# Chunked attention and a channel mix on one core: a new order for the steps of the opening

## The chip, the cores and the metric

The kernel runs on one core of a Trainium2 chip. The metric is the device time of one execution in microseconds (us). The kernel before takes 577.14 us by the median of three runs (576.09 to 577.93). The engines are TensorE (PE, with its weight loads as PEld), ScalarE (ACT), VectorE (DVE), GpSimd (POOL) and SyncE (SP, which here issues nearly all loads and stores).

## The reference

Inputs q, k, v have the shape batch 8, heads 8, sequence 576, head size 64. The sequence is cut into chunks of 64, and each chunk attends to itself alone:

```
scores = q_c @ k_c.T / sqrt(64)              # 64 x 64 for each chunk and head
attn   = softmax(scores)                     # sum + 1e-9 in the denominator
x      = (attn @ v_c), heads side by side    # 8 x 576 x 512
x_prev = x shifted by one token, zero at the start of a batch
xk     = mu_k * x + (1 - mu_k) * x_prev;   xr likewise with mu_r
k      = relu(xk @ w_k)                      # 512 -> 1024
v      = (k * k) @ w_v                       # 1024 -> 512
out    = sigmoid(xr @ w_r) * v
```

## The kernel before

The 8 x 576 tokens are 4608 in a row, cut into 18 groups of 256 and 36 tiles t of 128. Every product of the channel mix is made in three passes over a high and a low part of each operand (`PASSES`, L612), so activations and weights have to be split: hi is a rounded copy, lo is the rest. The attention of groups 0 to 2 and the channel mix of groups 0 and 1 are called the opening here; it is written tile by tile, because the weights are still on their way. The groups behind it run from another list (`GROUP`), which the change leaves alone.

**How the order is set.** Each function of the opening registers small steps under a task name (`do`, class `Steps`); a step is called task.number. The string `START` (from L27) lists all steps in one order, with an engine behind a colon where there is a choice, and the loop at L1210 issues them in that order. Within each engine, and within SP's queue, instructions keep the order of the text. Semaphores between engines, and the waits for a free buffer of a pool, follow from the data. The engine letter counts only in steps that copy, subtract or apply relu and square on either engine; the passes over weights have fixed engines. `W:n` issues n idle products on PE, which have no reader.

**The steps**, with the lines where they are defined:

- `nq`, `nk` (L173): a group's q or k into a ring, 512 KB, on SP. `v` (L191): a tile's v, four loads, two buffers. `bq3`, `bk3` (L208): 16 small loads each of q or k for group 3, by 32-blocks.
- `swk`, `swr`, `swv` (L271): load of 1 MB of weights. `cw...` 0 and 1 are two ScalarE passes over it, 2 a combine on VectorE (they turn the stored words into fp32); `hw...` 0 is the copy to the high part, 1 the low part (a subtraction). wk has four such blocks, wr two, wv four; wv2 and wv3 share one buffer for the loaded words.
- `mu`, `dg` (L230, L526): the mix factors, and 16 diagonal matrices made from them on ScalarE.
- `T`g (L348): 0, 2 transpose q's even and odd tokens on PE, 4, 6 k's; 1, 3, 5, 7 copy them to `qT`, `kT`. The products go to the pool `ps_k`, two buffers of one bank, which `K` and `mu` use too.
- `S`t (L384): 0 scores on PE, 1 maximum, 2 subtraction (both read PSUM on VectorE), 3 exponential on ScalarE, 4 sum, epsilon and reciprocal, 5 division. Two tiles share one PSUM buffer (`ps_s`, one buffer of two banks, which `P`.0 uses in turn), and steps that touch the same bank wait for each other in the order of the text.
- `P`t (L456): 0 transposes the probabilities on PE, 1 copies them out, 2 multiplies with v, 3 fills the shifted column, 4 copies the result x out.
- `Mk`t, `Mr`t (L542): 0 difference, 1 mix (for t = 0, 1, 2 on PE with the diagonals, in pool `ps_o`; else on VectorE), 2 high copy, 3 low part (`Mr` has no step 0: 0 mix, 1 high, 2 low).
- `K`gf (L618): 0 the product with a block of wk (24 products), 1 relu, 2 square, 3 high, 4 low. `R`gt (L673): 0 the product with wr, 1 sigmoid. `V`g... (L699): products with wv, one step for each of eight row blocks, and the last steps multiply with the sigmoid and store.
- `D6`, `D7` (L377): VectorE turns the q (0) and k (1) blocks of group 3.

The pools that matter: `ps_k` 2 buffers, `ps_s` 1, `ps_x` 1 (results of P.2 for two tiles), `ps_o` 2 (mixes, R and V).

Of the kernel before, what the change touches and what calls it, by code (L numbers as in the profile page):

```python
# [24 lines left out]


START = """  # L27
W:9 mu.0:A nq0.0 nk0.0 T0.0 T0.2 T0.1:A swr1.0 P0.3:D T0.3:A nk1.0 nq1.0 T0.4 T0.5:A swr0.0
T0.6 T0.7:A W:4 S0.0 S0.1:D S0.2:D S1.0 W:4 T1.4 S1.1:D v0.0 T1.6 S1.2:D cwr1.1:A S0.3:A S0.4:D
S0.5:D cwr1.0:A T1.5:A W:3 T1.0 S1.3:A S1.4:D S1.5:D P0.0 T1.7:A cwr1.2:D T1.2 cwr0.0:D P1.0  # L30
T1.1:A mu.1 P0.1:A T1.3:A cwr0.1:A nq2.0 P0.2 P1.1:A S2.0 T2.2 S3.0 P0.4:D P1.3:D S2.1:D v1.0
S2.2:D mu.2:A dg.0:A S3.1:D T2.0 swk0.0 S2.3:A cwr0.2:D Mk0.1 S3.2:D T2.3:A P1.2 S2.4:D
hwr1.0:A Mk1.0:D Mk0.0:D nk2.0 Mk0.2:A cwk0.0:A swk2.0 S2.5:D Mr0.0 swk1.0 cwk0.1:A P1.4:A
T2.1:A S3.3:A T2.6 Mr0.1:A hwr1.1:D Mk0.3:D P2.3:D hwr0.0:A P2.0 cwk0.2:D Mr0.2:D Mk1.1 swk3.0
Mk1.2:A Mk1.3:D T2.7:A hwr0.1:D T2.4 Mr1.0 hwk0.0:D P2.1:A Mr1.1:D hwk0.1:D R00.0 cwk2.0:A
Mr1.2:D v2.0 S3.4:D cwk1.1:A T2.5:A Mk2.0:D cwk1.0:A swv2.0 S3.5:D v3.0 cwk1.2:D cwk3.1:A P2.2
R01.0 P2.4:A cwk2.1:A K00.0 swv0.0 R00.1:A P3.3:D R01.1:A cwk3.0:A cwk2.2:D P3.0 P3.1:A K00.1:A
hwk2.0:A Mr2.0 P3.2 hwk1.0:A cwk3.2:D Mr2.1:A S4.0 P3.4:A Mk2.1 hwk2.1:D S5.0 hwk1.1:D cwv2.0:A
cwv2.1:A hwk3.0:A swv1.0 K01.0 K01.1:A K01.2:A Mk3.0:D Mr3.0:D K02.0 K00.2:A cwv2.2:D hwk3.1:D
v4.0 Mk3.1:D Mr2.2:D S4.1:D Mr3.1:A K03.0 cwv1.1:A Mr3.2:D cwv1.0:A bk3.0 Mk2.2:D Mk2.3:D  # L40
K00.3:A R10.0 S5.1:D Mk3.2:A cwv0.1:A K01.3:A hwv2.0:A K00.4:D K02.1:A K02.2:A K01.4:D K02.3:A
P4.3:D cwv0.0:A R10.1:A Mk3.3:D hwv2.1:D R11.0 K03.1:A K02.4:D K03.2:A R11.1:A K10.0 K10.1:A
swv3.0 K10.2:A cwv0.2:D K11.0 cwv1.2:D hwv0.0:A K03.3:A S4.2:D K13.0 hwv1.0:A hwv0.1:D cwv3.1:A
bq3.0 S5.2:D cwv3.0:A K10.3:A K03.4:D v5.0 hwv1.1:D V001.0 cwv3.2:D S4.3:A K13.1:A V001.1
V001.2 hwv3.0:A K10.4:D V001.3 V001.4 S4.4:D K13.2:A S4.5:D V001.5 P4.0 hwv3.1:D S5.3:A V001.6
V001.7 P4.1:A S5.4:D K13.3:A S5.5:D P4.2 K11.1:A K13.4:D D7.1:D v7.0 P5.0 P4.4:A K11.2:A
V001.8:D K12.0 V10.0 V001.9:D V11.0 K11.3:A V11.1 P5.1:A Mk4.0:D Mk4.1:D K12.1:A P5.2 K12.2:A
P5.3:D K12.3:A K11.4:D V10.1 D6.1:D K12.4:D P5.4:A Mr4.0:D V10.2 V10.3 V11.2 V11.3 Mk5.0:D
V10.4 Mk5.1:D Mr4.1:A V11.4 D7.0:D Mk4.2:A V10.5 v6.0 V10.6 V11.5 V10.7 Mk5.2:A Mk4.3:D Mr4.2:D
Mk5.3:D Mr5.0:D Mr5.1:A V11.6 D6.0:D V11.7 V11.8:D Mr5.2:D V10.8:D  # L50
"""


# [1255 lines left out]
```

## Time and profile before

| what | value |
|---|---|
| median of three runs | 577.14 us (576.09 to 577.93) |
| the profiled execution | 577.38 us |
| its span, first to last instruction | 575.6 us |
| granted clock of TensorE, mean | 0.999 |
| DMA over the span | 49.25 MB, mean 86 GB/s |

All rows are of the profiled execution. Times in rows count from the start of its span. A row of a timeline merges neighbouring instructions of one kind; the length of a merged row reaches to the end of its last instruction, so that rows of a pipelined PE overlap by a little, and the distance from one start to the next is the cost of a step in a full queue.

### The profile page before, as it was taken

The numbers are of one execution on the slowest core, as the hardware profiler recorded it, in microseconds if no ns is written. First come the engines' busy times: TensorE is split into PE (matmuls) and PEld (weight loads), VectorE is DVE, ScalarE is ACT, GpSimd is POOL, SyncE is SP. The second block draws the span as 40 slices with busy tenths as digits, with TensorE's granted clock in tenths as the row PEclk, the third lists the DMA queues.
The fourth block names the chain that finished last, engine by engine and source line by source line (L and its number), as shares of the span: only waits on it lengthen the run. The fifth ranks groups of instructions, "written<-read, shape, count | busy, mean of one in ns | idle before, by whom it ended". The sixth has DMA issues, their size and how long they took to land.

```text
span 575.6 us, 15305 instructions
## 1 busy us (share of the span) xinstructions
PE 566.6 (98%) x6485; PEld 535.8 (93%) x6485; DVE 453.8 (79%) x763; ACT 356.2 (62%) x535; POOL 0.7 (0%) x6
## 2 busy tenths in 40 slices
PE   7899999999999999999999999999999999999997
PEld 7779999999999999999999999999999999999997
DVE  1686878889888888888888697979798878876835
ACT  4898975473848383929292929292938384747462
POOL 0000000000000000000000000000000000000000
PEclk9999999999999999999999999999999999999999
DMA  9997342433443343434203434343434343010011
GB/s 286 201 315 199 89 86 75 89 67 70 69 91 66 82 69 88 70 91 67 72 1 90 68 86 69 84 71 89 69 83 69 84 70 74 21 41 36 1 38 38
DMA packets 184276, 49.25 MB, mean 86 GB/s; under 512 B 169608, under 2 KB 176272, under 8 KB 184208
## 3 DMA queue, kind: packets, MB, share of 16 engines
q1 hardware_dynamic: 183904, 48.01, 37.1%
q8 instruction: 51, 0.84, 0.6%
q10 hardware_dynamic: 304, 0.27, 0.1%
q14 instruction: 17, 0.14, 0.1%
HBM read 38.80 MB, written 9.44 MB: 84 GB/s over the span
## 4 chain that ended last, share of the span: by engine, by line
PE 95%; DMA 3%; ACT 0%; SPq 0%; DVE 0%; issue 0%
PE pk L627 35%; PE pr L680 17%; PE vx L900 15%; PE vyz L900 11%; PE pv L711 6%; PE xps L1085 3%; PE s L1011 3%; PE pt L1067 2%; DMA v<-in_v 2%; PE trq L358 1%; DMA q_ring<-in_q 1%; PE mxk L571 1%; PE s L401 1%; PE trk L358 1%; PE xps L485 1%; PE warm L1214 1%
## 5 line engine op out<-in xcount | busy, mean ns | idle before, releaser
L627 PE MATMUL pk<-xkhi,wk 128*128 128x256 f32 x1152 | 202.2, 278 | 0.0
L627 PEld LDWEIGHTS pk<-xkhi,wk 128*128 128x128 f32 x1152 | 175.4, 188 | 1.2
L627 PE MATMUL pk<-xklo,wk 128*128 128x256 f32 x576 | 159.4, 277 | 0.0
L647 ACT ACTIVATE rr<-pk 128x512 f32<-128x512 f32 x60 | 35.3, 588 | 128.6 <-PE pk L627 128.6
L627 PEld LDWEIGHTS pk<-xklo,wk 128*128 128x128 f32 x576 | 108.3, 188 | 0.1
L680 PE MATMUL pr<-wr,xrhi 128*128 128x512 f32 x288 | 90.4, 395 | 0.0
L900 PE MATMUL vyz<-b,kk 128*128 128x256 f32 x540 | 68.7, 276 | 0.0
L900 PE MATMUL vx<-b,ks 128*128 128x256 f32 x540 | 68.7, 276 | 0.0
L900 PEld LDWEIGHTS vx<-b,ks 128*128 128x128 f32 x540 | 64.7, 188 | 0.0
L900 PEld LDWEIGHTS vyz<-b,kk 128*128 128x128 f32 x540 | 64.7, 188 | 0.0
L680 PEld LDWEIGHTS pr<-wr,xrhi 128*128 128x128 f32 x288 | 52.7, 188 | 10.2
L680 PE MATMUL pr<-wr,xrlo 128*128 128x512 f32 x144 | 56.2, 390 | 0.0
L738 DVE TENSOR_TENSOR kk<-rr,kk 128x1024 fp32r<-128x1024 f32 x30 | 35.4, 1222 | 11.2 <-ACT kk L884 11.1
L654 ACT ACTIVATE rr<-rr 128x512 f32<-128x512 f32 x60 | 38.0, 633 | 1.9
L929 ACT ACTIVATE u<-vx 128x256 f32<-128x256 f32 x30 | 11.5, 384 | 42.3 <-PE vx L900 42.3
L711 PE MATMUL pv<-b,kk 128*128 128x256 f32 x288 | 33.9, 277 | 0.0
L711 PEld LDWEIGHTS pv<-b,kk 128*128 128x128 f32 x288 | 33.1, 188 | 0.1
L680 PEld LDWEIGHTS pr<-wr,xrlo 128*128 128x128 f32 x144 | 27.0, 188 | 5.7
L846 DVE TENSOR_TENSOR ss<-rr 128x512 f32<-128x512 f32 x15 | 10.4, 692 | 24.7 <-ACT rr L654 24.7
L738 DVE TENSOR_TENSOR ks<-ss,ks 128x512 fp32r<-128x512 f32 x45 | 28.3, 685 | 0.0
L1147 DVE SCALAR_TENSOR_TENSOR mk<-d,mu,x 128x256 f32<-128x256 f32 (+3 forms) x80 | 27.6, 413 | 0.4
L1147 DVE SCALAR_TENSOR_TENSOR mr<-d,mu,x 128x256 f32<-128x256 f32 (+3 forms) x80 | 27.6, 412 | 0.0
(127 smaller groups left out, 864.0 us busy)
## 6 DMA issues: line engine op xcount, KB each, us to landing
v<-in_v SPq DMA_DIRECT2D x144, 64.0 KB, 2.4
out<-sg SPq DMA_DIRECT2D x34, 256.0 KB, 2.6
q_ring<-in_q SPq DMA_DIRECT2D x192, 36.0 KB, 2.0
k_ring<-in_k SPq DMA_DIRECT2D x192, 36.0 KB, 2.0
wk_st<-in_moe_w_k SPq DMA_DIRECT2D x4, 1024.0 KB, 12.8
wv_st<-in_moe_w_v SPq DMA_DIRECT2D x4, 1024.0 KB, 7.4
wr_st<-in_moe_w_r SPq DMA_DIRECT2D x2, 1024.0 KB, 10.1
q_ring<-in_q SPq DMA_DIRECT2D x2, 512.0 KB, 6.7
```

The lines of the kernel that those rows point to most:

```text
L358: nc.tensor.matmul(x[halves[j], hp, :], T[f"{nm}{g}"][:, j * HP + hp, r, :], ident, start=True, stop=True,)
L627: nc.tensor.matmul(pk[:, e, :], wk[a][:, cb, f * P : (f + 1) * P], xk[b][:, cb, :], start=(n == 0), stop=(n == 3 * NB - 1),)
L647: nc.scalar.activation(r, T[f"pk{g}{fp}"], AF.Relu)
L654: nc.scalar.activation(r, r, AF.Square)
L680: nc.tensor.matmul(pr, xr[a][:, cb, tl * TT : (tl + 1) * TT], wr[b][:, cb, :], start=(n == 0), stop=(n == 3 * NB - 1),)
L711: nc.tensor.matmul(T[f"pv{g}{tl}"][:, cols[c]], kk[a][:, f, tok[tl]], quarter(f // HF, c)[:, b, f % HF, :], start=(f == 0 and n == 0 and c ...
L738: nc.vector.tensor_tensor(to, x, y, ALU.subtract)
L900: nc.tensor.matmul(to, a[i][:, f, :], weight(w, j, f), start=first and f == 0 and n == 0, stop=f == HF - 1 and n == 2, skip_group_check=True,)
L1011: nc.tensor.matmul(T[f"s{g}"][halves[e], j, tl, hp, :], qT[halves[j], hp, cols], kT[halves[j], hp, cols], start=True, stop=True,)
L1067: nc.tensor.transpose(out=T[f"pt{g}"][:, tl, hp, :], in_=T[f"pg{g}"][:, tl, 2 * hp : 2 * hp + 2, :], identity=ident,)
L1085: nc.tensor.matmul(T[f"xps{g}"][halves[c], 2 * j + a, tl * TT + e * CH : tl * TT + (e + 1) * CH], T[f"v{2 * g + tl}"][halves[j], hp, e, :] ...
L1147: nc.vector.scalar_tensor_tensor(out=to[:, cb, s : s + w], in0=T[f"d{g}"][:, cb, s : s + w], scalar=mu[:, cb : cb + 1], in1=T[f"xg{g}"][:, ...
```

## The change

Only the string `START` changes. It holds the same 292 steps and the same four `W` entries (9, 4, 4 and 3 products). Their order is new. Of the steps with a choice of engine, 23 go from ScalarE to VectorE (T0.5, T0.7, T1.1, T1.3, T2.5, P1.1, P2.4, P4.4, P5.1, hwk1.0, hwk3.0, hwv0.0, hwv1.0, hwv2.0, K01.1, K01.3, K02.1, K03.3, K10.2, K10.3, K11.1, Mr2.1, Mk3.2) and two from VectorE to ScalarE (hwk0.0, Mk2.2). On SP the order becomes nk0 nq0 wr1 nq1 nk1 wr0 v0 v1 nq2 wk0 nk2 wk1 wk2 v2 wk3 v3 wv0 wv2 wv1 bk3 wv3 v4 bq3 v5 v7 v6.

```diff
--- before.py
+++ after.py
@@ -25,29 +25,29 @@
 
 
 START = """
-W:9 mu.0:A nq0.0 nk0.0 T0.0 T0.2 T0.1:A swr1.0 P0.3:D T0.3:A nk1.0 nq1.0 T0.4 T0.5:A swr0.0
-T0.6 T0.7:A W:4 S0.0 S0.1:D S0.2:D S1.0 W:4 T1.4 S1.1:D v0.0 T1.6 S1.2:D cwr1.1:A S0.3:A S0.4:D
-S0.5:D cwr1.0:A T1.5:A W:3 T1.0 S1.3:A S1.4:D S1.5:D P0.0 T1.7:A cwr1.2:D T1.2 cwr0.0:D P1.0
-T1.1:A mu.1 P0.1:A T1.3:A cwr0.1:A nq2.0 P0.2 P1.1:A S2.0 T2.2 S3.0 P0.4:D P1.3:D S2.1:D v1.0
-S2.2:D mu.2:A dg.0:A S3.1:D T2.0 swk0.0 S2.3:A cwr0.2:D Mk0.1 S3.2:D T2.3:A P1.2 S2.4:D
-hwr1.0:A Mk1.0:D Mk0.0:D nk2.0 Mk0.2:A cwk0.0:A swk2.0 S2.5:D Mr0.0 swk1.0 cwk0.1:A P1.4:A
-T2.1:A S3.3:A T2.6 Mr0.1:A hwr1.1:D Mk0.3:D P2.3:D hwr0.0:A P2.0 cwk0.2:D Mr0.2:D Mk1.1 swk3.0
-Mk1.2:A Mk1.3:D T2.7:A hwr0.1:D T2.4 Mr1.0 hwk0.0:D P2.1:A Mr1.1:D hwk0.1:D R00.0 cwk2.0:A
-Mr1.2:D v2.0 S3.4:D cwk1.1:A T2.5:A Mk2.0:D cwk1.0:A swv2.0 S3.5:D v3.0 cwk1.2:D cwk3.1:A P2.2
-R01.0 P2.4:A cwk2.1:A K00.0 swv0.0 R00.1:A P3.3:D R01.1:A cwk3.0:A cwk2.2:D P3.0 P3.1:A K00.1:A
-hwk2.0:A Mr2.0 P3.2 hwk1.0:A cwk3.2:D Mr2.1:A S4.0 P3.4:A Mk2.1 hwk2.1:D S5.0 hwk1.1:D cwv2.0:A
-cwv2.1:A hwk3.0:A swv1.0 K01.0 K01.1:A K01.2:A Mk3.0:D Mr3.0:D K02.0 K00.2:A cwv2.2:D hwk3.1:D
-v4.0 Mk3.1:D Mr2.2:D S4.1:D Mr3.1:A K03.0 cwv1.1:A Mr3.2:D cwv1.0:A bk3.0 Mk2.2:D Mk2.3:D
-K00.3:A R10.0 S5.1:D Mk3.2:A cwv0.1:A K01.3:A hwv2.0:A K00.4:D K02.1:A K02.2:A K01.4:D K02.3:A
-P4.3:D cwv0.0:A R10.1:A Mk3.3:D hwv2.1:D R11.0 K03.1:A K02.4:D K03.2:A R11.1:A K10.0 K10.1:A
-swv3.0 K10.2:A cwv0.2:D K11.0 cwv1.2:D hwv0.0:A K03.3:A S4.2:D K13.0 hwv1.0:A hwv0.1:D cwv3.1:A
-bq3.0 S5.2:D cwv3.0:A K10.3:A K03.4:D v5.0 hwv1.1:D V001.0 cwv3.2:D S4.3:A K13.1:A V001.1
-V001.2 hwv3.0:A K10.4:D V001.3 V001.4 S4.4:D K13.2:A S4.5:D V001.5 P4.0 hwv3.1:D S5.3:A V001.6
-V001.7 P4.1:A S5.4:D K13.3:A S5.5:D P4.2 K11.1:A K13.4:D D7.1:D v7.0 P5.0 P4.4:A K11.2:A
-V001.8:D K12.0 V10.0 V001.9:D V11.0 K11.3:A V11.1 P5.1:A Mk4.0:D Mk4.1:D K12.1:A P5.2 K12.2:A
-P5.3:D K12.3:A K11.4:D V10.1 D6.1:D K12.4:D P5.4:A Mr4.0:D V10.2 V10.3 V11.2 V11.3 Mk5.0:D
-V10.4 Mk5.1:D Mr4.1:A V11.4 D7.0:D Mk4.2:A V10.5 v6.0 V10.6 V11.5 V10.7 Mk5.2:A Mk4.3:D Mr4.2:D
-Mk5.3:D Mr5.0:D Mr5.1:A V11.6 D6.0:D V11.7 V11.8:D Mr5.2:D V10.8:D
+P0.3:D W:9 nk0.0 nq0.0 T0.6 mu.0:A T0.4 T0.5:D swr1.0 T0.2 nq1.0 T0.0 T0.1:A T0.3:A W:4 T0.7:D
+S0.0 S0.1:D S0.2:D S0.3:A S0.4:D S1.0 S1.1:D S1.2:D W:4 W:3 nk1.0 T1.4 cwr1.1:A T1.6 S0.5:D
+S1.3:A P0.0 S1.4:D T1.0 cwr1.0:A T1.5:A cwr1.2:D swr0.0 v0.0 mu.1 T1.7:A S1.5:D P0.1:A P1.0
+cwr0.0:D cwr0.1:A T1.1:D T1.2 P0.2 P0.4:D T1.3:D S2.0 v1.0 P1.1:D P1.2 Mk1.0:D cwr0.2:D mu.2:A
+S3.0 S2.1:D dg.0:A S2.2:D nq2.0 T2.0 P1.3:D Mk0.1 Mk0.2:A Mk0.3:D swk0.0 S2.3:A hwr0.0:A S2.4:D
+S3.1:D S3.2:D nk2.0 swk1.0 swk2.0 Mr0.0 T2.2 T2.3:A cwk0.0:A v2.0 hwr1.0:A S2.5:D P2.0 cwk0.1:A
+P1.4:A Mk0.0:D hwr0.1:D Mr0.1:A S3.3:A hwr1.1:D T2.6 T2.7:A Mr0.2:D cwk0.2:D Mk1.1 Mk1.2:A
+swk3.0 P2.1:A hwk0.0:A Mk1.3:D T2.1:A T2.4 Mr1.0 Mr1.1:D R00.0 Mr1.2:D R01.0 S3.4:D hwk0.1:D
+S3.5:D cwk1.1:A cwk1.0:A cwk2.0:A cwk2.1:A P3.0 v3.0 P2.3:D swv0.0 P3.1:A cwk2.2:D P2.2
+cwk1.2:D P2.4:D K00.0 P3.2 hwk2.0:A R01.1:A R00.1:A T2.5:D S4.0 hwk1.0:D hwk2.1:D P3.3:D Mr2.0
+hwk1.1:D cwk3.1:A cwk3.0:A cwk3.2:D hwk3.0:D K00.1:A S5.0 K00.2:A P3.4:A Mk2.1 swv2.0 cwv2.0:A
+swv1.0 Mk3.0:D Mk2.0:D Mk3.1:D K01.0 K01.1:D K02.0 hwk3.1:D bk3.0 cwv2.1:A K01.2:A K03.0
+Mr2.1:D Mr2.2:D Mr3.0:D cwv2.2:D Mr3.1:A K01.3:D Mk2.2:A Mr3.2:D Mk2.3:D S4.1:D K00.3:A R10.0
+K00.4:D hwv2.0:D K02.1:D cwv1.1:A swv3.0 Mk3.2:D cwv0.1:A cwv1.0:A Mk3.3:D cwv0.0:A R11.0
+K01.4:D v4.0 S4.2:D hwv2.1:D K02.2:A K02.3:A K02.4:D K10.0 cwv1.2:D K03.1:A cwv0.2:D hwv0.0:D
+K11.0 R10.1:A K13.0 R11.1:A K10.1:A K10.2:D hwv0.1:D hwv1.0:D hwv1.1:D S5.1:D S4.3:A P4.3:D
+V001.0 K03.2:A S5.2:D cwv3.1:A cwv3.0:A cwv3.2:D hwv3.0:A K03.3:D K03.4:D K10.3:D V001.1 V001.2
+V001.3 V001.4 V001.5 S5.3:A S4.4:D S4.5:D P4.0 hwv3.1:D V001.6 V001.7 bq3.0 K13.1:A K13.2:A
+v5.0 K13.3:A K13.4:D S5.4:D S5.5:D P4.1:A V001.8:D D7.0:D P4.2 K12.0 P5.0 P4.4:D K11.1:D
+K10.4:D K11.2:A V001.9:D Mk4.0:D K12.1:A K12.2:A D7.1:D K11.3:A P5.1:D K11.4:D Mk4.1:D V10.0
+V10.1 V11.0 K12.3:A K12.4:D P5.3:D P5.2 P5.4:A Mk5.0:D Mr4.0:D Mr4.1:A Mk4.2:A V11.1 V10.2
+V11.2 V10.3 V10.4 V11.3 V11.4 V11.5 V11.6 V10.5 D6.1:D v7.0 Mr4.2:D Mk5.1:D V10.6 D6.0:D
+Mk5.2:A V10.7 Mk4.3:D Mk5.3:D Mr5.0:D Mr5.1:A V10.8:D V11.7 V11.8:D Mr5.2:D v6.0
 """
```

## Rows read from the trace of the kernel before

**Rows 1.** The page, part 1: busy time (share of the span) and instructions of TensorE, of its weight loads and of the other engines.

```profile
PE 566.6 (98%) x6485; PEld 535.8 (93%) x6485; DVE 453.8 (79%) x763; ACT 356.2 (62%) x535; POOL 0.7 (0%) x6
```

**Rows 2.** The table by stages (start:end and length in us, then busy time and instruction count of each engine, granted clock of TensorE, DMA share, GB/s): the opening from PE's first transposes to the first scores of group 3, and the groups behind it.

```profile
5.30:104.90 99.60, 95.23 (x1215) 88.14 (x1215) 70.58 (x133) 75.23 (x121) 0.00 (x0) 1.00 0.67 173
104.90:560.00 455.10, 455.10 (x5165) 432.27 (x5158) 374.58 (x615) 275.41 (x405) 0.00 (x0) 1.00 0.32 67
```

**Rows 3.** The waits of PE over the whole span: who waited <- who ended the wait: us in total, times, longest. This list is whole.

```profile
PE s L401 <- DVE p L421: 1.5, 1, 1.5
PE s L401 <- ACT pT L141: 1.3, 1, 1.3
PE warm L1214 <- DVE x L502: 1.1, 1, 1.1
PE mxk L571 <- ACT x L141: 0.5, 1, 0.5
PE xps L485 <- ACT pT L141: 0.5, 1, 0.5
PE trq L358 <- DMA q_ring<-in_q: 0.4, 1, 0.4
PE xps L485 <- DMA v<-in_v: 0.3, 1, 0.3
```

**Rows 4.** The timeline of PE in the opening: start and length in us, line, operation, output<-inputs, count; in brackets the idle time ahead and what ended it. In order: T0.0 and T0.2, T0.4 and T0.6, S0.0, T1.0, P0.0, P1.0, S2.0, Mk0.1, P1.2, Mr0.0, the first of R00, P2.2, the first of R01, the first of K01. x32 of `s` or `xps`, x16 of `trq` and of `mxk` are one step each.

```profile
5.34 1.97 PE L358 MATMUL trq<-ident,q_ring 128*64 128x128 f32 x32 [0.43 <-DMA q_ring<-in_q]
...
7.17 1.97 PE L358 MATMUL trk<-ident,k_ring 128*64 128x128 f32 x32
...
10.15 0.69 PE L401 MATMUL s<-kT,qT 64*64 64x64 f32 x32
...
16.86 1.09 PE L358 MATMUL trq<-ident,q_ring 128*64 128x128 f32 x16
...
17.89 0.66 PE L465 MATMUL pt<-ident,p 128*128 128x128 f32 x4
...
19.50 0.66 PE L465 MATMUL pt<-ident,p 128*128 128x128 f32 x4
...
22.86 0.69 PE L401 MATMUL s<-kT,qT 64*64 64x64 f32 x32 [1.33 <-ACT pT L141]
...
26.16 2.05 PE L571 MATMUL mxk<-x,diag_k 128*128 128x128 f32 x16
...
28.14 0.69 PE L485 MATMUL xps<-pT,v 64*64 64x64 f32 x32
...
28.77 2.05 PE L571 MATMUL mxr<-x,diag_r 128*128 128x128 f32 x16
...
37.78 0.71 PE L680 MATMUL pr<-wr,xrhi 128*128 128x512 f32 x2
...
41.07 1.65 PE L485 MATMUL xps<-pT,v 64*64 64x64 f32 x32 [0.27 <-DMA v<-in_v]
...
42.64 0.72 PE L680 MATMUL pr<-wr,xrhi 128*128 128x512 f32 x2
...
54.35 0.38 PE L627 MATMUL pk<-xkhi,wk 128*128 128x256 f32 x1
```

**Rows 5.** The chain that ended last, in order of time (start, length, what): the first load, and the last of the loads of v for the third tile.

```profile
0.73 4.47 DMA q_ring<-in_q
...
31.61 10.49 DMA v<-in_v
```

**Rows 6.** The timeline of ScalarE (ACT), same columns: T1.5, S1.3, P1.1, the first eight diagonals, two passes over a block of wk.

```profile
15.31 0.65 ACT L141 ACTIVATE kT<-trk 128x512 f32<-128x512 f32 x1 [1.27 <-PE trk L358]
...
15.84 0.61 ACT L425 ACTIVATE p<-p 128x512 f32<-128x512 f32 x1
...
22.20 0.61 ACT L141 ACTIVATE pT<-pt 128x512 f32<-128x512 f32 x1
...
22.97 2.45 ACT L536 ACTIVATE diag_k<-ident,mu 128x128 f32<-128x128 f32 x8
...
30.19 1.19 ACT L296 ACTIVATE wk_st<-wk_st 128x1024 f32<-128x1024 f32 x1
...
31.27 1.16 ACT L300 ACTIVATE wk_st<-wk_st 128x1024 int32<-128x1024 uint32 x1
```

**Rows 7.** The timeline of VectorE (DVE), same columns: S0.1, S0.2, the sum of S1.4 (its two small steps follow within the distance to the next row), S1.5, a combine of a weight block, P0.4.

```profile
10.92 0.69 DVE L413 TENSOR_REDUCE m<-s 128x8 f32<-128x512 f32 x1 [9.91 <-PE s L401]
...
11.64 0.69 DVE L421 TENSOR_TENSOR p<-s,m 128x512 f32<-128x512 f32 x1
...
16.48 0.69 DVE L429 TENSOR_REDUCE z<-p 128x8 f32<-128x512 f32 x1 [0.15 <-ACT p L425]
...
17.64 0.69 DVE L435 TENSOR_TENSOR p<-p,z 128x512 f32<-128x512 f32 x1
...
18.25 1.22 DVE L303 SCALAR_TENSOR_TENSOR wr_st<-wr_st 128x1024 int32<-128x1024 int32 x1
...
21.60 0.69 DVE L143 COPY x<-xps 128x512 f32<-128x512 f32 x1 [2.13 <-PE xps L485]
```

**Rows 8.** The timeline of SyncE's queue (SP): how long it took to issue v1 (four loads) and bq3 (sixteen).

```profile
14.16 6.74 SPq L199 DMA_DIRECT2D v<-in_v  x4
...
68.40 10.52 SPq L221 DMA_DIRECT2D q_ring<-in_q  x16
```

## The prediction, made before the change was run

> **What bounds the kernel now.** I read the page first: TensorE (PE) is busy for 566.6 of 575.6 us [rows 1]. The table by stages then says where the rest is: from 104.9 to 560 us PE does not idle at all; between 5.3 and 104.9 us it idles 4.37 us [rows 2]. The list of PE's waits names each gap: 1.5 us before scores S1.0, 0.5 before P0.2, 1.3 before S2.0, 0.5 before Mk1.1, 0.3 before P2.2, and 0.4 for the first keys or queries [rows 3]. One more is hidden in busy time: P2.2 lasts 1.65 us where the same 32 products start 0.63 us ahead of their successor elsewhere (28.14 to 28.77) [rows 4]; its values, issued behind the wk loads on SP's queue, land 10.49 us after the last issue [rows 5]. P2.2 to R01 takes 1.57 (41.07 to 42.64), 0.94 more than 0.63; with the 0.27 of idle ahead of it that load costs 1.2 us. PE's work is the same before and after (292 steps, the same 20 idle products in W), so the change is worth what it does to these gaps: at most 4.37+0.94 = 5.3 us can be won, and each new wait is lost in full, since PE has no slack behind to absorb it [rows 2]. All times below are of the profiled execution (577.38 us, 0.24 over the median 577.14).
>
> **The method.** On each engine instructions run in the order of the text: P1.1's input was there by 20.2 us, but ScalarE did T1.3 and a weight pass first and reached it at 22.20, and S2.0 waited for it [rows 3, 4, 6]. So I walk the new order with the old durations. A ScalarE copy out of PSUM takes 0.6 to 0.65 us, 0.53 from start to start; a weight pass 1.16 to 1.19, 1.08 from start to start [rows 6]. VectorE takes 0.69 for a 128x512 step (0.61 start to start, 0.72 where the next needs its result), 1.16 for the sums, epsilon and reciprocal of step S.4, 1.22 for a weight combine [rows 7]. On PE a q or k half (T) goes 1.03, a score or values step 0.63, a mix (Mk, Mr) 1.98 [rows 4].
>
> **Part 1, first transposes.** The pool of T has two buffers. Before, T0.4 followed T0.1's copy; now T0.6, T0.4, T0.2, T0.0 stand ahead of all copies but one in the text, so T0.2 needs T0.5 and T0.0 needs T0.7, both now on VectorE. T0.4 ends as the second half did, at 5.34+1.97 = 7.31 [rows 4]; T0.5 runs 7.35 to 8.04, T0.7 to 8.65; T0.2 starts 8.08, T0.0 9.05 and ends 10.1; T0.1 10.1 to 10.75, T0.3 to 11.25. W:4 lies within this. S0.0 starts at 11.25, not 10.15: **+1.1**. The loads (k ahead of q, q1 ahead of k1) cost nothing: both first loads were in by 7.17, and the swapped second ones are wanted only at 16. VectorE copying a transposed tile with its strided store is not in the trace. Nearest rows: 0.69 for its copy of xps, upper end 1.22 for a VectorE step of twice the elements [rows 7], lower end ScalarE's 0.53 start to start [rows 6]. I take 0.69, the same 128x512 out of PSUM. Four such copies lie on the path (T0.5, T0.7, T1.1, T1.3): -0.6 to +2.1 us for the range.
>
> **Part 2, to S2.0.** S1.0 waits for S0.2 as before (1.5). S0.4 now stands ahead of S1.1 on VectorE and waits for the exponential; behind it S1.1, S1.2, S0.5 end at 17.3, and the seven W products and T1.4, T1.6 (to 17.95) cover that, about 1.1 us if they did not. S1.3 follows at 16.75, the pass cwr1.0 to 18.4, and only then T1.5 (18.95), whose buffer T1.0 needs: PE waits 0.45. S1.4, cwr1.2 and S1.5 end at 20.4 (P1.0 waits 0.3), T1.1 at 21.0, releasing T1.2; P0.2 22.05 to 22.7; P0.4, ahead of T1.3 and P1.1 on VectorE, holds both: they end at 23.4, 24.05, 24.65. S2.0 needs T1.3 and P1.1 and starts at 24.7 against 22.86 [rows 4]: 1.84, that is **+0.74** on top of part 1. The new wait there is 2.0 us and replaces 0.5 and 1.3.
>
> **Part 3, to R00.** PE: S2.0, P1.2, S3.0, T2.0, Mk0.1 from 27.6 to 29.6, Mr0.0, T2.2 to 32.6. The diagonals on ScalarE (8 in 2.45 us [rows 6], 16 from 22.2 to 27.1) are in time. But S2.3 stands behind Mk0.2 on ScalarE (29.7), and S2.4, S3.1, S3.2, S2.5 behind Mk0.3 on VectorE (30.3 to 31.0): S2.5 ends at 34.1 and P2.0 waits 1.5 us. On ScalarE T2.3 waits for T2.2 (32.65), then come cwk0.0, hwr1.0, cwk0.1, and only at 36.4 P1.4, whose input has lain there since 26: done at 36.95. T2.6 ends at 35.7, so Mk1.1 waits 1.25 us. Before, Mk1.1 waited 0.5 [rows 3]. R00 starts at 41.95 against 37.78 [rows 4]: 4.17, so this part gives **+2.3**.
>
> Loads here: v1 now goes ahead of q2. Its issue took SP 6.74 us, to 20.9 [rows 8], with the queue's earlier loads landing meanwhile; q2 behind it should be issued by then and, with the 4.47 us that the very first load took [rows 5], be there by 26; T2.0 wants it at 26.6. Lower bound nothing, upper bound about 2 us if it lands as late as it would with wk0 in front; I take nothing. v2 now goes ahead of wk3, and P2.2 comes behind R01 and P3.0, at 48: its 1.2 us go.
>
> **Part 4, R00 to K01.** Before 54.35-37.78 = 16.57 us [rows 4], less 1.2 = 15.4; I find no new wait (K00's weights at 45.7, wanted at 48.9; the sigmoids free Mr2.0's buffer at 51.7, wanted at 52.9). K01 starts at 57.3 against 54.35: **+2.9** in all (1.1+0.74+2.3-1.2).
>
> **Part 5, behind K01.** The order on PE is nearly the old one, with no idle before. 23 copies go from ScalarE to VectorE and 2 back: at most 21 x 0.69 = 14.5 us more on an engine busy 70.6 of 99.6 us [rows 2], so it fits, with less cover. My walk finds hwk3.1 (behind K01.1, which waits for PE at 60.0) done 0.9 us ahead of K03, Mk3.3 0.6 ahead of K10, hwv0.1 1.1 ahead of V001.0, hwv3.1 0.3 ahead of V001.6, and P5.1 0.3 late for P5.2. On SP bq3 (10.52 us of issue [rows 8]) now stands behind swv3 and v4, while D7.0, which reads it, comes ahead of P4.2 and not behind V11.4, with P4.4, K11.1 and K10.4 queued behind it. I take **+0.5** (the 0.3 and a little), between nothing and 2.5.
>
> Sum: 577.38+2.9+0.5 = 580.8 for a profiled execution; less 0.24, **580.5** by the median.
>
> **Rivals.** (a) *Later covers run out too*: VectorE reaches D7.0 at about 91.5, the query blocks land only later, and V10.0, which needs K10.4, stands. For it: margins of 0.3 to 1.1 us above. Against it: each is still a margin, and P4.0 to P5.2 leave PE other work. 1 to 2.5 us more: 581.5 to 583.0. It decides if bq3's last load lands after 91.5.
> (b) *The other side: ScalarE and VectorE take what is ready first*, at P1.4, S2.3 and P1.1. Then P1.4 runs near 27, S2.3 at 28.2, and 2.75 us of part 3's waits go: 577.8; if P1.1 and T1.3 pass P0.4 too, S2.0 starts near 22.8 and 1.9 more go: 575.9. It decides at P1.4: a start before 35.1 and Mk1.1 has no wait. Against it stands P1.1 at 22.20 [rows 6]. Into its chance I put any other way in which these waits come out shorter than walked.
> (c) *The clock.* PE's longest gap in the stage was 1.5 us, and the granted clock stayed at 1.00 there, the 2.4 GHz level [rows 2, 3]; the gap ahead of S2.0 would be 2.0, with two of over 1 us soon behind it. If the clock fell to the 1.2 GHz level, the 2.9 us of work from S2.0 to Mk0.1 would take 2.9 more: 583.4. The Trainium skill (TensorE: Matmul & The Clock Gate, What's actually happening) has idleness throttle the array to half rate and speaks against an order with more gaps; by it this rival's price would be that doubling of whatever runs until the clock is back, while no run here shows a fall inside the kernel's work.
>
> **How the numbers follow.** A measurement of this kernel tells about 0.3% (1.7 us) from no change, so faster is below 575.4 and slower above 578.9. My walk has 0.62 (of that 0.05 within the bound, if the margins of parts 1 to 3 all come out low), (a) 0.14, (b) 0.20 (0.12 same, 0.08 faster), (c) 0.04. So slower 0.75, same 0.17, faster 0.08. The range goes from 577.0 (inside (b)) to 583.0 (the strided copies' upper end, or (a)'s).
>
> **What would show it.** Right: S0.0 near 11.2, S2.0 near 24.7 with VectorE's P1.1 as its releaser, P2.0 behind VectorE's S2.5 near 34, Mk1.1 waiting for ScalarE's x near 37, no wait for v2, K01 near 57.3, and PE's idle between 5.3 and 105 us up by about 3 us. Wrong: S2.0 before 23.5, P1.4 before 35, or PE without idle between 25 and 42. Should K01 come near 57 and the end still be under 578, it would be my claim that PE absorbs nothing behind K01 that failed.

## The result, and the profile after

The changed kernel takes **584.13 us** by the median of four runs (581.66 to 585.11), the kernel before beside it 576.83: ratio 1.012 [1.008, 1.016]. A second measurement gave 585.02, ratio 1.015 [1.013, 1.016]. It is slower, as forecast, but by 7.3 us and not by 3.4, above the top of the range (583.0). The profiled execution is the one of 585.11, with a span of 583.3 us: 7.7 more than before. "Mean clock" below is the mean granted clock that each run reports.

The page, part 1 (against [rows 1]) and the row of part 3 for the instructions that the engines fetch:

```profile
PE 569.2 (98%) x6485; PEld 538.7 (92%) x6485; DVE 465.5 (80%) x788; ACT 342.8 (59%) x510; POOL 0.7 (0%) x6
...
q8 instruction: 51, 0.84, 0.6%
```

The table by stages, the opening and the rest (against [rows 2]):

```profile
5.30:112.00 106.70, 96.89 (x1179) 90.14 (x1183) 81.93 (x157) 61.66 (x96) 0.00 (x0) 0.97 0.59 159
112.00:568.00 456.00, 456.00 (x5210) 433.11 (x5201) 375.17 (x617) 275.93 (x407) 0.00 (x0) 1.00 0.32 68
```

PE still never idles behind the opening; in it it idles 9.8 us instead of 4.4, and the granted clock is 0.97, not 1.00. PE's waits (against [rows 3]), without the last two, of 0.4 and 0.2 us:

```profile
PE s L401 <- DVE pT L143: 2.1, 1, 2.1
PE s L401 <- issue: 2.0, 1, 2.0
PE pt L465 <- DVE p L435: 1.8, 2, 1.6
PE s L401 <- DVE p L421: 1.5, 1, 1.5
PE warm L1214 <- DVE x L502: 1.1, 1, 1.1
PE mxk L571 <- ACT x L141: 1.0, 1, 1.0
PE trq L358 <- DVE kT L143: 0.8, 1, 0.8
```

Four of them are waits that the prediction walked: T0.2 for a copy (0.8), S2.0 for VectorE's P1.1 (2.1), P2.0 for S2.5 (1.6), Mk1.1 for ScalarE's x (1.0). The second, 2.0 us with "issue" for a releaser (the hole, below), is not: no engine and none of the kernel's loads ended it. The timeline of PE (against [rows 4]): T0.6 and T0.4, S0.0, S2.0, S3.0 in two pieces with the hole between, T2.0, Mk0.1, Mr0.0, P2.0, Mk1.1, P2.2, the first of K01:

```profile
5.19 2.54 PE L358 MATMUL trk<-ident,k_ring 128*64 128x128 f32 x32
...
11.73 0.69 PE L401 MATMUL s<-kT,qT 64*64 64x64 f32 x32 [0.15 <-ACT qT L141]
...
25.12 0.69 PE L401 MATMUL s<-kT,qT 64*64 64x64 f32 x32 [2.10 <-DVE pT L143]
...
26.07 0.39 PE L401 MATMUL s<-kT,qT 64*64 64x64 f32 x10
28.45 0.91 PE L401 MATMUL s<-kT,qT 64*64 64x64 f32 x22 [1.99 <-issue]
29.29 1.97 PE L358 MATMUL trq<-ident,q_ring 128*64 128x128 f32 x16
31.20 3.24 PE L571 MATMUL mxk<-x,diag_k 128*128 128x128 f32 x16
34.27 1.95 PE L571 MATMUL mxr<-x,diag_r 128*128 128x128 f32 x16
...
38.85 0.63 PE L465 MATMUL pt<-ident,p 128*128 128x128 f32 x4 [1.61 <-DVE p L435]
...
41.55 2.05 PE L571 MATMUL mxk<-x,diag_k 128*128 128x128 f32 x16 [1.05 <-ACT x L141]
...
52.45 0.69 PE L485 MATMUL xps<-pT,v 64*64 64x64 f32 x32
...
61.51 0.36 PE L627 MATMUL pk<-xkhi,wk 128*128 128x256 f32 x1
```

T2.0 lasts 1.97 us for [rows 4]'s 1.09, Mk0.1 3.24 for 2.05: that is the clock. The same stretch in windows of 1 us (columns as in [rows 2]: the third figure from the end is the granted clock):

```profile
26.00:27.00 1.00, 0.46 (x29) 0.33 (x22) 0.10 (x1) 1.00 (x5) 0.00 (x0) 0.94 1.11 213
27.00:28.00 1.00, 0.00 (x0) 0.00 (x0) 0.00 (x0) 0.25 (x1) 0.00 (x0) 0.50 1.15 240
...
32.00:33.00 1.00, 1.00 (x6) 1.00 (x6) 0.00 (x0) 0.00 (x0) 0.00 (x0) 0.50 1.06 387
33.00:34.00 1.00, 1.00 (x8) 1.00 (x7) 0.00 (x0) 0.00 (x0) 0.00 (x0) 0.64 1.16 280
34.00:35.00 1.00, 1.00 (x11) 1.00 (x11) 0.00 (x0) 0.53 (x2) 0.00 (x0) 1.00 1.29 202
```

From 27 to 33 us PE's clock stood at 0.50, its 1.2 GHz level. What it did before: 2.1 us of waiting, S2.0, P1.2 and ten products; the fall came ahead of most of the hole. ScalarE's P1.4 and VectorE's P1.1 and S2.5 stood in their queues where the walk put them. The timeline of ScalarE (against [rows 6]), P1.4:

```profile
40.92 0.58 ACT L141 ACTIVATE x<-xps 128x512 f32<-128x512 f32 x1
```

The timeline of VectorE (against [rows 7]), P1.1 and S2.5:

```profile
24.29 0.68 DVE L143 COPY pT<-pt 128x512 f32<-128x512 f32 x1
...
38.03 0.68 DVE L435 TENSOR_TENSOR p<-p,z 128x512 f32<-128x512 f32 x1
```

**Where the 7.7 us of the two profiled executions lie**, by starts on PE: to S0.0 +1.58; S0.0 to S2.0 +0.68 (13.39 for 12.71); S2.0 to R00 +6.33 (R00 46.37); R00 to K01 -1.43; behind K01 +0.55.

### The profile page after: what moved, and what is told of

Its sections match the earlier page's. It is cut to its first block, busy times and chain, and to the rows that moved or that the text cites. A ratio compares the mean times of both kernels' runs of the same rounds, so it can differ in the third digit from the quotient of the medians.

```text
span 583.3 us, 15302 instructions
## 1 busy us (share of the span) xinstructions
PE 569.2 (98%) x6485; PEld 538.7 (92%) x6485; DVE 465.5 (80%) x788; ACT 342.8 (59%) x510; POOL 0.7 (0%) x6
## 4 chain that ended last, share of the span: by engine, by line
PE 96%; DVE 1%; ACT 1%; issue 1%
PE pk L627 34%; PE pr L680 17%; PE vx L900 15%; PE vyz L900 11%; PE pv L711 6%; PE xps L1085 3%; PE s L1011 3%; PE pt L1067 2%; PE mxk L571 1%; PE trq L358 1%; PE mxr L571 1%; PE warm L1214 1%; PE xps L485 1%; PE s L401 1%; PE trk L358 1%
```

## The experiments

In the changed kernel e1 to e5, e10 and e15 take the hole, the fall and the waits apart; e8 and e9 split the change; e6, e7 and e11 to e14 try what can be mended, in either order. Theory W: the walked waits make about 3 us, the hole and the fall of the clock the rest. Rivals: D, the copies now on VectorE cost it, late behind K01; O, the walk is wrong and the order costs it elsewhere. In each diff a minus line is where a step stood in `START`, a plus line where it stands. Three dots mark steps left out. Ratios are against the kernel before in the same series; its median is 575.76 beside e1 to e4 and 577.2 to 577.4 beside the others (e13 shows why), so ratios of different series compare to about 0.3%.

| kernel | median us | ratio |
|---|---|---|
| after again | 585.02 | 1.0146 [1.0130, 1.0163] |
| v2 ahead of wk0 (e1) | 581.41 | 1.0089 [1.0071, 1.0107] |
| fill ahead of S2.0 (e2) | 581.76 | 1.0100 [1.0080, 1.0120] |
| P1.4 earlier (e3) | 581.65 | 1.0096 [1.0071, 1.0121] |
| first transposes of before (e4) | 579.98 | 1.0069 [1.0043, 1.0095] |
| both mends (e10) | 580.05 | 1.0060 [1.0047, 1.0074] |
| fill alone, thrice (e15) | 581.80 | 1.0089 [1.0073, 1.0104] |
| waits mended (e6) | 577.47 | 1.0014 [1.0002, 1.0026] |
| new engines alone (e8) | 581.69 | 1.0072 [1.0053, 1.0090] |
| new order alone (e9) | 588.42 | 1.0200 [1.0184, 1.0217] |
| before, v2 earlier (e7) | 576.45 | 0.9994 [0.9983, 1.0005] |
| before, nine steps (e11) | 577.04 | 1.0006 [0.9993, 1.0018] |
| before, four steps (e12) | 575.99 | 0.9988 [0.9979, 0.9997] |
| before again (e13) | 577.21 | 1.0004 [0.9992, 1.0017] |
| before, filled (e14) | 576.76 | 0.9998 [0.9988, 1.0007] |

**e1: fewer loads beside S3.0.**

```diff
+v2.0
 swk0.0
...
-v2.0
 hwr1.0:A
```

> The changed kernel with the load of v2 moved ahead of wk0, k2, wk1, wk2 on SP's queue: since v2 waits for P0.2, the large loads start only behind 23 us. Theory F: the 2.0 us hole inside S3.0 is PE waiting for its next 16 KB of instructions, which come through the same DMA engines and stood behind the weight loads; with the queue quiet from 20 to 23 us the block comes earlier and the hole goes: -2.0. If the clock fell because of this hole (theory C2), it stays at 1.00 too, another -2.4: about 579.7; if it fell because of the 2.1 us wait ahead of S2.0 alone (C1), about 582.1. Rival G, a wait on data that the profile doesn't show: hole and time stay, 584.

The hole is gone, S2.0 still waits 2.10, and the clock still fell behind that wait:

```profile
25.00:26.00 1.00, 1.00 (x76) 1.00 (x71) 0.67 (x1) 1.00 (x5) 0.00 (x0) 0.86 0.44 98
26.00:27.00 1.00, 1.00 (x31) 0.88 (x25) 0.25 (x1) 0.83 (x3) 0.00 (x0) 0.50 0.89 117
...
29.00:30.00 1.00, 1.00 (x10) 1.00 (x10) 0.00 (x0) 0.00 (x0) 0.00 (x0) 0.93 1.04 390
```

So the wait alone is enough for a fall, and without the hole the low stretch is half as long. One of the four runs has a mean clock of 1.000 and takes 580.42, the other three 581.4 to 581.6.

**e2: the wait ahead of S2.0 filled.**

```diff
+W:12
 S2.0
```

> The changed kernel with 12 idle products (about 1.6 us) on PE ahead of S2.0, where it waits 2.1 us. No step moves. C1 (that wait lowers the clock): the granted clock stays at 1.00 behind it, -2.4, about 581.7. C2 (the hole in S3.0 lowers it): the clock falls as before, 584. Theory F: a hole of about 2 us stays, reached 48 instructions sooner in the order of the work; theory G: it stays at the same place in S3.0.

Clock 1.00 from the first scores on, and no hole: there theories F and G both missed, since each had it stay. But the fill ran 23.16 to 26.03, 0.7 to 0.9 us longer than the wait, and gave that much back. One of the four runs still has a mean clock of 0.997.

**e3: P1.4 sooner.**

```diff
+P1.4:A
 Mk0.2:A
...
-P1.4:A
 Mk0.0:D
```

> The changed kernel with P1.4 moved ahead of Mk0.2 on ScalarE, into a stretch of 7 us in which that engine is idle. By my walk the wait of Mk1.1 (1.05 us) goes and nothing else changes: 583.1. If the wait ends with something else than P1.4's place, 584.1.

Mk1.1's wait is gone from the list. In its profile the clock fell elsewhere, 14.3 to 17.7 us, behind S1.0's 1.5 us wait, and the hole was 0.3. Two of the four runs have a mean clock of 0.996 (580.3 and 580.9), two 0.994 (582.4 and 582.8), so the median says little of the wait itself. Where the fall comes is not the order's alone.

**e4: the first transposes and loads as before.**

```diff
+mu.0:A nq0.0 nk0.0 T0.0 T0.2 T0.1:A swr1.0 T0.3:A nk1.0 nq1.0 T0.4 T0.5:A T0.6 T0.7:A
-nk0.0 nq0.0 T0.6 mu.0:A T0.4 T0.5:D swr1.0 T0.2 nq1.0 T0.0 T0.1:A T0.3:A
...
-T0.7:D
...
-nk1.0
```

> The changed kernel with the first transposes and their copies (T0) and loads in the order and on the engines of before. By my walk S0.0 starts 1.1 us earlier, and by the two profiles 1.6 us (11.73 against 10.15): 582.5 to 583. If the clock's rise at the start is what cost 0.5 of it, S0.0 starts between 10.15 and 10.7 depending on when the clock rises. If the delay is absorbed behind S0.0, 584.1.

S0.0 at 10.11, part 1's +1.1 back. S2.0 waits the same 2.10 us, and this time the clock stayed at 1.00: by the runs' mean clocks it fell in two of five (580.5 and 582.5; the others 579.0 to 580.0).

**e5: the changed kernel again**, nothing edited.

> The changed kernel once more, on the chip of the runs beside it. Theory (late instruction block and clock, both a matter of chance in each execution): runs spread over 2 to 4 us, from about 580 without hole and fall to about 584.5 with both; in the profile S0.0 between 11.2 and 11.8, S2.0 13.4 us behind it, and K01 at 57.5 to 61.7, later by just the hole and the half-clock stretch. Rival (a fixed loss): every run within 0.3% of the median and the hole in S3.0 in this profile too.

Its profiled run, 581.8, is the shortest of five (the others 584.2 to 585.6). The hole:

```profile
25.56 0.69 PE L401 MATMUL s<-kT,qT 64*64 64x64 f32 x32 [2.10 <-DVE pT L143]
...
26.51 0.39 PE L401 MATMUL s<-kT,qT 64*64 64x64 f32 x10
27.08 0.57 PE L401 MATMUL s<-kT,qT 64*64 64x64 f32 x22 [0.17 <-issue]
```

0.17 us for 1.99, ahead of the same product, the eleventh (in e3 it is 0.34 there, in e9 0.88). The second of the packets that bring PE instructions in the opening (queue q8, 16 KB each) ends at 26.76 in after, at 25.50 here and at 19.84 in before: it came late where PE stood without an instruction. In all four profiles with the hole the eleventh product starts 1.5 to 1.7 us behind the end of that packet (28.45 behind 26.76, here 27.08 behind 25.50). The packet was late in starting, not slow (1.37 us in after, 1.29 in before): it began 3.1 us behind the start of P0.2 in after, 1.9 in e3, 1.7 here, 0.9 in e9, and within 0.2 us of it in e1, e2, e4 and e10, which have no hole. Why it starts late is open: from 22 to 23 us the DMA share was 1.12 in e2 and 1.06 in after.

The clock fell at 14.5 here. All nine runs of the changed kernel, the four of the result and these five, have a mean clock below 1: seven 0.993 or 0.994, as the profile of after, and the two shortest (581.66 and 581.8) 0.997, with the low stretch half as long in the profile here.

**e10: both mends at once.**

```diff
+W:8
 S2.0
...
+v2.0
 swk0.0
...
-v2.0
 hwr1.0:A
```

> The changed kernel with both mends at once: v2 moved ahead of wk0 (the hole in S3.0 goes) and 8 idle products ahead of S2.0, about 1.3 us of the 2.1 us wait there. If hole and clock are the whole of what the walk did not have, what is left is the walk: 577.4 + 2.9, less nothing: 579.5 to 580.8, ratio 1.004 to 1.006, granted clock 1.00 from 20 to 40 us, S2.0 still at 25.1. If the fill only moves the fall of the clock to another place, 581.5 as with either mend alone.

580.05, as theory W has it. The eight idle products are x16 in the row (each stands as two) and filled 2.05 us, not 1.3:

```profile
22.43 2.05 PE L1214 MATMUL warm<-idle 128*128 128x128 f32 x16
24.59 0.69 PE L401 MATMUL s<-kT,qT 64*64 64x64 f32 x32
25.08 0.68 PE L485 MATMUL xps<-pT,v 64*64 64x64 f32 x32
25.55 0.68 PE L401 MATMUL s<-kT,qT 64*64 64x64 f32 x32
26.15 1.09 PE L358 MATMUL trq<-ident,q_ring 128*64 128x128 f32 x16
27.18 2.05 PE L571 MATMUL mxk<-x,diag_k 128*128 128x128 f32 x16
```

No hole, no slow row; R00 at 41.18, K01 at 56.36. S2.0 to R00 takes 16.6 us, 4.7 less than in after: the price of hole and clock together. Of the 5.1 us between the two profiles 0.5 lie ahead of S0.0 and these 4.7 here; every other stretch agrees within 0.1.

**e15: the fill without the earlier v2.**

```diff
+W:8
 S1.0
...
+W:8
 S2.0
...
+W:6
 P2.0
```

> The changed kernel with idle products in its gaps (8 ahead of S1.0, 8 ahead of S2.0, 6 ahead of P2.0) and v2 left where the change puts it, so that only the clock is mended and not the hole. If the clock stays at 1.000 and the hole is left: 580 to 582 by whether the hole of 0 to 2 us comes, ratio 1.006 to 1.009. If fill takes the hole away too (the next instructions are fetched sooner), 579.7 to 580.3 as with both mends.

Clock 1.00 and no hole, but 581.8. The last fill costs it: the idle products write one of the two buffers of `ps_o`, and keeping that past Mr0.0 makes Mr0.0 wait 1.4 us for Mk0.3. So the run does not part the two costs cleanly; it shows the hole gone with v2 left in place.

**e8 and e9: one half of the change each.** e8 has before's order with the new engine letters; e9 has the new order with the old letters, except for T0.5 and T0.7.

```diff
-... T1.1:A P1.1:A ... K01.1:A K02.1:A hwk3.0:A ...
+... T1.1:D P1.1:D ... K01.1:D K02.1:D hwk3.0:D ...
```

> The order of before with the engines of the change (23 copies to VectorE, 2 to ScalarE), nothing moved. My walk: P1.1 then runs on VectorE at about 20.8 and not behind a weight pass at 22.2, so S2.0's 1.3 us and P0.2's 0.5 go; about -1.5 at K01, 574.3, and nothing lost later. Rival: VectorE (14.5 us more work) is late behind K01 and PE idles there: 576 or more.

> The new order with the old division of copies: of the 25 steps whose engine changed only T0.5 and T0.7 stay on VectorE (with them on ScalarE the order of the opening closes into a circle). If the order alone makes the loss, it is all still here: the steps that stand behind others in the text (P1.1 behind P0.4, S2.3 behind Mk0.2, P1.4 behind a weight pass) still wait, K01 starts near 58 and the time is 581 to 584, ratio 1.007 to 1.013, by whether the hole of up to 2 us and the fall of the clock come in its run. If the division made a part of it (T1.1, T1.3 and P1.1 on VectorE), S2.0 comes before 24.5 and the time is 579 to 580.

e8's opening is quicker than before's (S2.0 at 22.25 with no wait, K01 at 52.71), and then VectorE is late with weights: PE waits 1.9 us for wk, 1.3 for wv. e9 loses 11 us; behind K01 it is ScalarE that is late. PE's waits in e8:

```profile
PE pk L627 <- DVE wk L314: 1.9, 1, 1.9
...
PE pv L711 <- DVE b L314: 1.3, 2, 1.1
```

PE's waits in e9:

```profile
PE pk L627 <- ACT relu L647: 3.4, 2, 2.2
```

So rival D is true of the letters alone and false of the change: order and letters fit each other. From K01 to the end each alone takes 6 us more than before (527.1 and 527.9 for 521.3), the two together 0.5. Of each 6, PE's waits are 3.5 and 3.7, which neither walk had (e8's rival did); behind one of them the clock fell (at 61.5 us in e8, behind 1.9; at 83.7 in e9, behind 2.2). e8's two runs at a mean clock of 1.000 take 579.3 and 579.8, the four at 0.997 581.6 to 582.3.

**e6: the waits of the walk mended**, in the changed kernel: the first transposes as in e4, T1.5 and T1.7 ahead of cwr1.0, cwr1.2 behind S1.5, P1.1 and T1.3 ahead of P0.4, S2.3 and P1.4 ahead of Mk0.1, Mk0.3 behind S2.5.

```diff
+P1.1:D T1.3:D
 P0.4:D
...
+P1.4:A
 Mk0.1
...
-Mk0.3:D
...
 S2.5:D
+Mk0.3:D
```

> The changed order and its division of copies, with the places mended where my walk found a wait: first transposes as before; T1.5, T1.7 ahead of cwr1.0; cwr1.2 behind S1.5; P1.1 and T1.3 ahead of P0.4; S2.3 and P1.4 ahead of Mk0.2; Mk0.3 behind S2.5. My theory (these waits are what the order cost, and nothing behind K01 costs): only S1.0's 1.5 and a few tenths at S2.0 stay, K01 starts at 51 to 52 and the whole takes about 573, 2 to 3 us under the kernel before. Rival (later covers, VectorE's extra copies): K01 comes as early, but PE idles behind it and the time is 575 or more.

S2.0 at 22.79 with 0.2 us of wait, Mk1.1 at 32.19 with none; but T2.4 now waits 1.6 us for T2.7 and T1.2 0.7 for T1.3. About half of what was mended came back as waits at the next copy in a queue: K01 starts at 53.81, and the median is 577.5 for a walked 573.

**e7: before with v2 ahead of wk3.**

```diff
+v2.0
 swk3.0
...
-v2.0
 S3.4:D
```

> The kernel before with one step moved: the load of v2 ahead of wk3 on SP's queue, as the change has it. If P2.2's stall is wk3's 1 MB in front of v2, it goes: -1.2. If v2 is late because its buffer is freed late or because the loads share the engines anyway, no difference.

P2.2's wait is gone from the profile and K01 is 1.33 us earlier (53.02), yet the ratio is 0.9994 [0.9983, 1.0005].

**e13: before again**, nothing edited; the question was whether the late v2 belongs to the kernel.

> The kernel before, unchanged, with a new profile. So far its runs fall in two groups: 575.6 to 576.4 with a mean granted clock of 1.000 and 576.8 to 577.6 with 0.997, while the profile behind the forecast has 0.999, 575.6 us of span and a late v2 (1.2 us). If the late v2 belongs to the kernel, a new profile shows P2.2 waiting for it again, whatever its clock, and a run at 1.000 has a span of 575 to 576. If it belonged to that one execution, P2.2 has no wait (0.63 to its successor), K01 comes near 53.1 and the span is 574 at a clock of 1.000; or, at 0.997, about 1.6 more behind a gap of the opening, where the windows of the granted clock show 0.50.

It does not: P2.2 starts at 42.30 with no wait and no load is in the list. And at a mean clock of 0.997 this is before with a fall of its own, behind a wait of 1.3 us:

```profile
23.00:24.00 1.00, 0.76 (x29) 0.76 (x32) 0.00 (x0) 0.97 (x6) 0.00 (x0) 0.68 1.05 410
24.00:25.00 1.00, 1.00 (x22) 0.88 (x18) 0.00 (x0) 1.00 (x5) 0.00 (x0) 0.50 1.05 377
...
26.00:27.00 1.00, 1.00 (x36) 0.81 (x32) 0.00 (x0) 1.00 (x5) 0.00 (x0) 0.62 1.20 233
```

The 35 runs of before in this series part in the same way: 15 at 1.000 take 575.5 to 576.6, 19 at 0.997 take 577.1 to 578.2, one at 0.999 576.5.

**e11, e12, e14: can before be beaten?** e11 moves T1.1, T1.3 and P1.4 to VectorE, P0.1 and P1.1 ahead of wr0's passes, S3.0 ahead of T2.2, v2 ahead of wk3 and wr0's copies ahead of wk0's passes. e12 moves four steps and no letter:

```diff
+P1.1:A
 cwr0.1:A
...
+P1.4:A
 cwk0.0:A
...
+hwr0.0:A
 cwk0.1:A
...
+v2.0
 swk3.0
```

e14 adds only fill:

```diff
+W:8
 S1.0
...
+W:3
 P0.2
...
+W:6
 S2.0
```

> The kernel before with its own waits mended by the same kind of step: v2 ahead of wk3 on the queue; T1.1, T1.3 and P1.4 on VectorE, where it is idle; P0.1 and P1.1 ahead of the weight passes of wr0 on ScalarE; S3.0 ahead of T2.2; the high and low part of wr0 ahead of the passes over wk0. By the walk S2.0 comes at 21.0 to 21.5 without a wait (before 22.86), Mk0.1 at 24.7 behind the diagonals, Mk1.1 without its 0.5, R00 at 35.5 to 36.5 (37.78), K01 at 51 to 52 (54.35): 574 to 575.5, ratio 0.994 to 0.997. If the saved time comes back as waits for weights behind R00 (the loads of wk and their passes are not sooner), 576 to 577.

> The kernel before with four steps moved and no engine changed: v2 ahead of wk3 on the queue; on ScalarE P1.1 ahead of the second pass over wr0, P1.4 ahead of the first pass over wk0, the high copy of wr0 ahead of the second. S2.0's wait falls from 1.3 to about 0.3, Mk1.1's 0.5 and v2's 1.3 go, R00 near 36.3 (or at 36.8 if it waits for wr's low part), K01 near 52: 574.5 to 575.5, ratio 0.995 to 0.997. If waits come back behind, 576 to 577.

> The kernel before with idle products in its own gaps and no step moved: 8 ahead of S1.0 (1.16 us of the 1.5 there), 3 ahead of P0.2, 6 ahead of S2.0. If the gaps are what lets the clock fall in half of its runs, all runs are at 1.000 and 575.6 to 576.4: ratio 0.997 to 0.999 against a mixed before. If the fall comes whatever the gaps hold, the two groups stay: ratio 1.000.

e11 gained 1.3 us at S2.0 and lost 2.3 in a new wait of Mk1.1, behind which its clock fell. e12 cut S2.0's wait to 0.3, but Mk1.1's went from 0.5 to 0.7 and Mr1.0 found a new one of 0.6; all its 12 runs are at 1.000, 575.7 to 576.6, which is what before does at 1.000. Its 0.12% is the clock's and no wait's. e14 held the clock too (11 of 12 runs at 1.000), but its fills, a third longer than the waits, put S2.0 0.8 us back.

## Why the prediction was wrong in size

**Part 1 held.** S0.0 at 11.16 and 11.21 in e5 and e10, 1.0 to 1.1 behind [rows 4], and e4 gave it back. After's own 11.73 has 0.5 more, because the clock rose later: T0.6 and T0.4 took 2.54 for 1.97, and the trace's first record of the full clock begins at 6.41, in [rows 4]'s execution at 4.40. That differs from run to run in before too (S0.0 at 10.55 in e13). The strided copies took 0.68 and 0.69, the value taken.

**Part 2 held.** +0.68 for +0.74; the wait 2.1 for 2.0, with P1.1 its releaser.

**Part 3's waits held** (1.6 for 1.5 at P2.0, 1.05 for 1.25 at Mk1.1), and its sum was 0.6 too high: S2.0 to R00 is 16.6 in e10 against 14.9 in [rows 4], +1.7 for +2.3. Half of that is S2.0, P1.2 and S3.0, which take 1.56 us together in e10 (24.59 to 26.15) for a walked 1.89. v1 ahead of q2 cost nothing, as taken. But this part had no term for the hole of 2.0 us: the walk counted engines and loads, and nothing else that could hold PE.

**Part 4's -1.2 is no gain of the change.** R00 to K01 is 15.14 for a walked 15.4; but in e7 it is 15.3, and 15.3 in e13 with nothing moved. No run of before at a mean clock of 1.000 takes over 576.6, where one with the late v2 would take about 577, so most runs of before don't have it either. The term only took back what the one profiled execution had in its 577.38. At a mean clock of 1.000 before takes about 575.8 (nine of the 23 runs beside e10, 575.6 to 576.4) and e10 580.0 (four runs, 579.7 to 580.1): the change's waits cost 4.2 us, measured as 1.05 + 0.68 + 1.67 + 0.55 = 3.95. That the forecast, 580.5, is near e10's time and not after's shows what it lacked: 4.7 us of hole and clock, less the fall that half of before's runs have as well. That it is so near is in part chance: it set out from 577.14, 1.4 above the 575.8, and added 3.4 for 4.2.

**Part 5: the size, not the place.** +0.55 behind K01 for +0.5, but no wait is listed there and P5.2 did not wait. By starts on PE, up to the first scores of group 3, 0.20 us of it lie in the products over wk (19.88 for 19.68) and 0.42 in those over wv (22.76 for 22.34), the same in e10; why they run slower stays open. So that the term came out is chance: it was put on P5.2.

**What failed is rival (c)'s chance, with its price left out of the sum, and the hole, which no term had.** (c) came behind the wait it named, on S3.0, T2.0 and Mk0.1, and with about the size given: 0.4, 0.9 and 1.1 make 2.4 us for 2.9. It had 0.04, and all nine runs of the changed kernel have a mean clock of 0.997 or less. The reason given against it, that PE's longest gap was 1.5 us and the clock stayed at 1.00, rested on one execution at 0.999. e13 shows the unchanged kernel falling behind 1.3 us, and the three times of before, 576.09 to 577.93, had shown a spread of 1.8 us, about what this fall makes (575.8 at 1.000 and 577.5 at 0.997, medians beside e10). By the Trainium skill (TensorE: Matmul & The Clock Gate, What's actually happening) idleness brings the array to half its rate. The trace agrees in the rate, 0.50 from 27 to 33 us; PE had waited 2.1 us, with work on both sides of the wait. That a wait of 2.10 brought it in e1 and not in e4 is shown by these runs only.

Rival (a) fell: bq3's last load landed at 92.4, but VectorE came to D7.0 only at 95.5 and did not wait. (b) fell at its own mark, P1.4 at 40.92. The hole was in no rival. It is tied to the fetch of PE's instructions by its place, by the releaser "issue" and by the packet on q8, whose end it follows by 1.5 to 1.7 us in four profiles. That the loads make the packet late is not shown: e1 and e10 thinned the loads and lost the hole, but e2, e4 and e15 lost it too, with v2 left where it was.

## What to carry to other kernels

Walking each engine's queue in the order of the text gave the waits that it found to 0.1 or 0.2 us, but it also missed some: e6, e8, e9 and e11 came out 1.5 to 7 us slower than walked. And a profile is one execution: before a stall is credited or a clock called safe, look at the spread of the kernel's times and at the clock of each run. Where an order leaves PE waits of one or two microseconds close together, price the fall of the clock and a late instruction fetch as likely, and test an order together with the engine letters it was made for.

## What the runs showed of the hardware

- PE's granted clock fell to 0.50 behind waits of 1.3 (before), 1.5 (e3, e5), 1.9 (e8), 2.1 (after, e1), 2.2 (e9) and 2.3 us (e11), with work just ahead and just behind. It stayed up behind 1.3 us (e7), 1.5 (e1) and 2.1 (e4) in other profiles. A fall cost 1.0 (e5) to 2.4 us (after).
- The clock's first rise differs from run to run: S0.0 came at 10.15 and 10.55 in two profiles of before, and from 11.16 (e5) to 11.95 (e2) in the changed order.
- PE stood 2.0, 0.9 (e9), 0.3 and 0.2 us inside a row of 32 products that had all their inputs, at the eleventh product, till 1.5 to 1.7 us behind the end of a 16 KB packet of its instructions that had begun late; in after this stood among loads of 310 GB/s (25 to 34 us).
